# Decode attention with a gated MLP: Wq loaded as two halves on two DMA queues, with x in three pieces behind the second

## The chip, the core and the metric

The kernel runs on one core of a Trainium2 chip. A core has five engines with instruction queues of their own: TensorE (PE, with PEld for its weight loads), VectorE (DVE), ScalarE (ACT), GpSimd (POOL) and SyncE (SP). SyncE and ScalarE issue the DMAs here; each has a DMA queue, q1 for SyncE and q10 for ScalarE in the profile, and both are served by the same 16 DMA engines. The metric is the device time of one execution in microseconds. The time before is 197.39 us, the median of three runs (197.38 to 197.52).

## The reference

Eight sequences, one new token each, D = 512. The token is layer-normalised; then a grouped-query attention (32 query heads, 8 KV heads of 128) over the last W = 2048 positions of a cache of 8192, and a gated MLP, both from the same normalised token. The output joins them.

```python
xn = _layernorm(x, axis=-1)
# attention: Hq = 32, Hkv = 8, Dh = 128, W = min(4096, max(256, Sk // 4)) = 2048
q = (xn @ wq)                                   # 8 x 4096
scores = einsum("bhqd,bhkd->bhqk", q, k[last W]) * Dh ** -0.5
o = einsum("bhqk,bhkd->bhqd", softmax(scores), v[last W])
s = o @ wo
# MLP, F = 1792
h = sigmoid(xn @ w_gate) * (xn @ w_up)
g = silu(h @ w_down)
return x + s * g
```

All tensors are bfloat16. Everything that is read is read once: Wq 4 MB, the windows of K and V 32 MB each, the MLP weights 5.25 MB, Wo 4 MB, and x, which is 8 KB.

## The kernel before

The order of the instructions on each engine is the order of the program text; nothing is rescheduled. An engine works through its instructions in that order and stops at the first whose inputs are not there.

**Loads.** All large loads are issued by SyncE through the helper `load` (L115), each as one DMA over 128 partitions: Wq with 32 KB per partition, each of the eight K tiles (4 MB) with 32 KB per partition, each of the sixteen V tiles (2 MB) with 16 KB. The tiles live in two rings. The K ring (`KRING = 3` buffers) holds, in this order, Wq, K0 to K7, the gate and up weights, the down weights and Wo; the V ring has four buffers for V0 to V15. `issue_loads()` issues loads in a fixed order (K0 to K6, V0, V1, K7, V2, ...) for as long as the next one's buffer has been released. At the start it issues K0 and K1 right after Wq. K2 takes Wq's buffer, which is released after the projection (L436); K3 takes K0's, released after the last `qk` of K0; K4 takes K1's, and so on.

**x.** Before any of this ScalarE issues x in four pieces of 128 columns (L124 to L128): eight rows of 256 bytes each.

**From x to the first K tile.** VectorE casts x (L240), takes mean and variance (L242, L244), ScalarE takes the root (L248), VectorE scales (L253), PE transposes (L263), VectorE copies the transposed token (L281), and PE multiplies it with Wq in 32 matmuls (L401). `q_out(0)` then lays the first half of q out in `qz_sb`: a cast on ScalarE (L415), a 32x32-block transpose on VectorE (L420), and small copies on both (L430, L432). Two clears of 0.48 us follow on VectorE (L450 and L648).

**The loop.** For each step t, `k_turn(t)` transposes one eighth of a K tile in place on VectorE (L460), eight steps to a tile; `qk(t - 4)` multiplies it with `qz_sb` on PE (L475). After step t = 1 `q_out(1)` lays out the second half of q. After every tile VectorE takes a maximum (L489), and after four tiles comes a softmax. From t = 52 the products with V (`pv`, L605) run beside it. All `k_turn`s stand behind `q_out(0)` on VectorE, so K0 can be transposed only when x has gone through the whole chain above.

**The end.** The MLP runs late, in the gaps. Wo is loaded last, in six pieces (the last of 128 KB), each multiplied as it lands (L719); two vector operations and the output DMA close the kernel (L730 to L734).

In the profile the tiles `x2_ps` and `x2_sb` appear as `x_ps` and `x_sb`, since the numbers of buffers are left out of names.

Of the kernel before, what the change touches and what calls it, by code (L numbers as in the profile page):

```python
# [10 lines left out]
def kernel(  # L11
# [14 lines left out]
    P = 128  # L26
    B, _, D = A_x.shape
    _, Hkv, Sk, Dh = A_k_cache.shape
    Hq = A_wq.shape[1] // Dh
# [3 lines left out]
    KT = D // P  # L33
# [76 lines left out]
    queues = [nc.sync, nc.scalar]  # L110

    def load(dst, src, q=None):
        if q is None:
            q = nc.sync
        q.dma_start(out=dst, in_=src)  # L115

    def k_tile(shape, name):
        return kring.tile(shape, bf16, name=name, tag="kring", align_bytes=ALIGN)

    def v_tile(shape, name):  # L120
        return vring.tile(shape, bf16, name=name, tag="vring", align_bytes=ALIGN)

    x_bf = work.tile([B, D], bf16, name="x_bf")
    for c in range(4):  # L124
        nc.scalar.dma_start(
            out=x_bf[:, P * c : P * (c + 1)],
            in_=A_x.flatten_outer_dims()[:, P * c : P * (c + 1)],
        )  # L128

    wq_sb = k_tile([P, KT, Hq * Dh], "wq_sb")  # L130
    load(wq_sb[:], A_wq.rearrange("(p kt) n -> p kt n", kt=KT))

    k_tiles = {}
    v_tiles = {}
# [77 lines left out]
    def issue_loads():  # L212
# [36 lines left out]
        out=rstd[:], in_=mv[:, 1:2], func=AF.Sqrt, bias=eps_t[:], scale=1.0  # L249
# [4 lines left out]
        out=xn_bf[:],  # L254
# [7 lines left out]
    for kt in range(KT):  # L262
        nc.tensor.transpose(  # L263
            out=xnT_ps[:, kt, :], in_=xn_bf[:B, kt::KT], identity=ident[:B, :B]
        )
    x2_ps = psum1.tile([NCOL * 32, DC], f32, name="x2_ps", tag="misc")
    for c in range(NCOL):
# [18 lines left out]
        out=HR[:],  # L286
        in_=ident[:].rearrange("m (h q r) -> m h r q", q=NQ, r=rep),
# [6 lines left out]
        out=Qm[:],  # L294
        in_=ident[:].rearrange("m (h q r) -> m q h r", q=NQ, r=rep),
# [6 lines left out]
        out=Hm[:],  # L302
        in_=ident[:].rearrange("p (a gl) -> p gl a", gl=GL),
# [6 lines left out]
    for j in range(GL):  # L310
        for gg in range(NG):
            g = NG * gg + j // 2
            nc.gpsimd.tensor_copy(
                out=spread[:, gg, j % 2, :, j], in_=ident[:, 32 * g : 32 * g + PP]
# [5 lines left out]
        out=rows_of[:],  # L320
        in_=ident[:].rearrange("p (a m) -> p m a", m=w),
# [5 lines left out]
        out=Sel[:], in_=rows_of[:].rearrange("p (g c r) -> p c g r", g=GL, c=NCH)  # L327
# [5 lines left out]
    for gg in range(NG):  # L333
        rows = slice(32 * gg, 32 * (gg + 1))
        cols = slice(NE * GL * rep * gg, NE * GL * rep * (gg + 1))
        for e in range(NE):
            nc.gpsimd.tensor_copy(
                out=pick[rows, e, cols].rearrange("p (h d) -> p h d", d=NE)[:, :, e],
                in_=ident[rows, 32 * gg : 32 * gg + GL * rep],
# [393 lines left out]
    for c in range(NCOL):  # L733
        queues[c].dma_start(  # L734
            out=out.flatten_outer_dims()[:, DC * c : DC * (c + 1)],
            in_=y_bf[32 * c : 32 * c + B, :],
# [31 lines left out]
```

## Time and profile before

| | us |
|---|---|
| median of three runs | 197.39 |
| the profiled execution's own time | 197.33 |
| its span (first to last instruction) | 195.5 |
| PE busy | 100.9 (52%) |
| VectorE busy | 105.5 (54%) |
| ScalarE busy | 31.0 (16%) |
| x issued / cast by VectorE | 0.73 / 12.93 |
| Wq issued / landed | 0.74 / 13.04 |
| projection (L401) | 15.96 to 19.45 |
| K0 landed / first transpose | 22.63 / 22.66 |
| last V products start | 179.7 |
| output issued | 193.25 |

The span leaves out some 1.8 us of the execution's own time, at its two ends. Times inside the span count from its start. The part of the profile with the span in 40 slices gives busy shares in tenths, the mean busy share of the 16 DMA engines, and what they moved. A DMA packet in the records is one row of a transfer (a partition's contiguous bytes) or one 4-byte completion marker; each of the engines that takes part in a DMA writes a marker behind its rows.

### The profile page before, as it was taken

How to read it: one execution, taken by the hardware profiler on the slowest of the kernel's cores; microseconds unless marked ns; L12 is line 12 of the kernel's file. 1: busy time of each engine (PE TensorE's matmuls, PEld its weight loads, DVE VectorE, ACT ScalarE, POOL GpSimd, SP SyncE). 2: the span in 40 equal slices, each digit the busy share in tenths (PEclk: the TensorE clock that was granted, in tenths of full speed). 3: DMA queues.
4: the chain of work that ended last, by engine and by line, in shares of the span. 5: the costliest groups of instructions: out<-in, count | busy, mean ns of one | idle time of the engine just before them, and what ended most of it. 6: DMA issues, size and time to landing. Idle time of an engine off the chain costs nothing.

```text
span 195.5 us, 1889 instructions
## 1 busy us (share of the span) xinstructions
PE 100.9 (52%) x750; PEld 36.4 (19%) x750; DVE 105.5 (54%) x149; ACT 31.0 (16%) x69; POOL 4.6 (2%) x25
## 2 busy tenths in 40 slices
PE   0008014434333248503793989868636862585663
PEld 0002001111001012101120223321312121232452
DVE  0025899999899999999959725413100010040401
ACT  2002450000000084000011134521111114011000
POOL 8000000000000000000000000000000000000000
PEclk9999855555555556755596699999987999589969
DMA  6999999999999999999999999999999999999991
GB/s 228 430 436 442 436 456 449 429 436 427 422 442 429 429 429 429 396 422 466 429 412 432 429 429 432 427 429 429 436 429 432 432 416 438 434 425 432 423 383 34
DMA packets 5000, 81.14 MB, mean 415 GB/s; under 512 B 624, under 2 KB 896, under 8 KB 1152
## 3 DMA queue, kind: packets, MB, share of 16 engines
q1 hardware_dynamic: 4912, 81.01, 97.0%
q8 instruction: 6, 0.10, 0.2%
q10 hardware_dynamic: 80, 0.01, 0.0%
q14 instruction: 2, 0.02, 0.0%
HBM read 81.01 MB, written 0.01 MB: 414 GB/s over the span
## 4 chain that ended last, share of the span: by engine, by line
DMA 65%; DVE 19%; PE 12%; issue 1%; SPq 1%; DVEq 0%
DMA k_sb<-in_A_k_cache_dram 31%; DMA wo_sb<-in_A_wo_dram 17%; DMA v_sb<-in_A_v_cache_dram 17%; DVE k_sb L460 16%; PE acc_ps L605 5%; PE s_ps L475 3%; PE a_ps L719 3%; PE pT_ps L536 1%; DVE pt_bf L523 1%; SPq L115 1%; DVE mx L489 1%; DVE qz_sb L430 0%; DVE qT_sb L420 0%; DVE prod L730 0%; DVE y_bf L732 0%
## 5 line engine op out<-in xcount | busy, mean ns | idle before, releaser
L460 DVE STREAM_TRANSPOSE k_sb<-k_sb 128x1024 f32<-128x1024 f32 x64 | 73.7, 1210 | 3.4 <-DMA k_sb<-in_A_k_cache_dram 3.4
L475 PE MATMUL s_ps<-k_sb,qz_sb 128*32 128x512 bf16 x256 | 30.4, 576 | 51.0 <-DVE k_sb L460 45.2
L605 PE MATMUL acc_ps<-v_sb,pT_sb 128*64 128x512 bf16 x256 | 36.6, 417 | 11.2 <-DMA v_sb<-in_A_v_cache_dram 11.2
L640 DVE TENSOR_TENSOR o_sb<-o_ps,rden 16x512 bf16<-16x512 f32 (+2 forms) x6 | 3.0, 504 | 47.6 <-PE o_ps L631 47.6
L619 ACT COPY acc_sb<-acc_ps 128x512 f32<-128x512 f32 x16 | 9.4, 585 | 83.9 <-PE acc_ps L605 83.9
L475 PEld LDWEIGHTS <-qz_sb 128*32 128x32 bf16 x256 | 8.6, 117 | 75.4 <-issue 51.7
L605 PEld LDWEIGHTS <-pT_sb 128*64 128x64 bf16 x256 | 12.7, 114 | 31.2 <-DMA v_sb<-in_A_v_cache_dram 15.4
L631 PE MATMUL o_ps<-acc_sb,Sel 128*16 128x512 f32 (+2 forms) x48 | 16.3, 490 | 3.4 <-ACT acc_sb L619 3.4
L557 DVE TENSOR_SCALAR pT_sb<-pc_bf,Hm 128x1024 bf16<-128x1024 bf16 x16 | 6.6, 477 | 4.8 <-PE acc_ps L605 4.7
L263 PE MATMUL xnT_ps<-ident,xn_bf 8*128 8x8 bf16 x4 | 0.3, 175 | 15.4 <-DVE xn_bf L253 15.4
L503 ACT ACT_TABLE_LOAD x1 | 1.3, 1283 | 39.7 <-DVE nm L497 39.7
L240 DVE CAST x_f<-x_bf 8x512 f32<-8x512 bf16 x1 | 0.4, 415 | 12.9 <-DMA x_bf<-in_A_x_dram 12.9
L489 DVE TENSOR_REDUCE mx<-s_ps 128x1 f32<-128x512 f32 x8 | 5.3, 662 | 3.8 <-PE s_ps L475 3.8
L631 PEld LDWEIGHTS o_ps<-acc_sb,Sel 128*16 128x16 f32 x48 | 4.7, 105 | 14.0 <-issue 8.1
L719 PE MATMUL a_ps<-wo_sb,o_sb 128*32 128x256 bf16 x64 | 5.2, 328 | 2.9 <-DMA wo_sb<-in_A_wo_dram 2.8
L536 PE MATMUL pT_ps<-pt_bf,spread 128*128 128x512 bf16 x16 | 5.8, 479 | 1.2 <-DVE pt_bf L523 0.7
L432 ACT COPY qz_sb<-qT_sb 32x32 bf16<-32x32 bf16 x20 | 4.8, 241 | 4.8 <-DVE qT_sb L420 4.5
L351 PE MATMUL d_ps<-wgu_sb,xnT_sb 128*32 128x448 bf16 x32 | 2.6, 463 | 5.6 <-DMA wgu_sb<-in_B_w_up_dram 3.3
L503 ACT ACTIVATE p_bf<-s_ps,nm 128x512 bf16<-128x512 f32 x8 | 5.4, 685 | 0.0
L544 ACT CAST pc_bf<-pT_ps 128x512 bf16<-128x512 f32 x8 | 4.6, 585 | 4.3 <-DVE pt_bf L523 2.8
L719 PEld LDWEIGHTS <-o_sb 128*32 128x32 bf16 x64 | 4.3, 116 | 3.8 <-issue 3.2
L523 DVE STREAM_TRANSPOSE pt_bf<-p_bf 128x512 bf16<-128x512 bf16 x8 | 4.9, 666 | 0.0
(59 smaller groups left out, 38.8 us busy)
## 6 DMA issues: line engine op xcount, KB each, us to landing
k_sb<-in_A_k_cache_dram SPq DMA_DIRECT2D x8, 4096.0 KB, 19.6
v_sb<-in_A_v_cache_dram SPq DMA_DIRECT2D x16, 2048.0 KB, 16.6
wq_sb<-in_A_wq_dram SPq DMA_DIRECT2D x1, 4096.0 KB, 12.3
wo_sb<-in_A_wo_dram SPq DMA_DIRECT2D x1, 2048.0 KB
wgu_sb<-in_B_w_gate_dram SPq DMA_DIRECT2D x1, 1792.0 KB
wgu_sb<-in_B_w_up_dram SPq DMA_DIRECT2D x1, 1792.0 KB
wd_sb<-in_B_w_down_dram SPq DMA_DIRECT2D x1, 1792.0 KB
wo_sb<-in_A_wo_dram SPq DMA_DIRECT2D x1, 1024.0 KB, 34.8
```

The source lines that it names most:

```text
L432: nc.scalar.copy(out=out, in_=in_)
L460: nc.vector.transpose(out=kw, in_=kw)
L475: nc.tensor.matmul(s_tiles[i][32 * g : 32 * (g + 1), :], lhsT=qz_sb[:, hb, h, 2 * a + e, :], rhs=kT[:, :, a, h, :, e], start=(n == 0), sto ...
L489: nc.vector.reduce_max(out=mx_of[hb][:, kq : kq + 1], in_=s_tiles[i][:], axis=AX.X)
L503: nc.scalar.activation(out=p_bf[:, :, kq], in_=s_tiles.pop(NK * hb + kq)[:].rearrange("p (o c j) -> p c j o", o=2, j=NC), func=AF.Exp, bia ...
L523: nc.vector.transpose(out=pt[:, w * n : w * (n + 1)], in_=p_bf[:, w * n : w * (n + 1)])
L536: nc.tensor.matmul(pT_ps[:], lhsT=spread[:, gg, y].rearrange("p k g -> p (k g)"), rhs=pt[:, c, y, :], start=(y == 0), stop=(y == 1), skip_ ...
L557: nc.vector.tensor_scalar(out=pT_of[hb, gg][:, :, gl, :], in0=pc, scalar1=Hm[:, gl : gl + 1], scalar2=None, op0=ALU.mult,)
L605: nc.tensor.matmul(acc_tiles[i][w * c : w * (c + 1), :], lhsT=pT[:, GL * rep * ch : GL * rep * ch + w], rhs=v_tiles[i][:, ch : ch + NCH, : ...
L619: nc.scalar.copy(out=acc_sbs[i // NSUM][:, i % NSUM], in_=acc_tiles.pop(i)[:])
L631: nc.tensor.matmul(o_ps[rows, :n, :], lhsT=Sel[:, c].rearrange("p g r -> p (g r)"), rhs=acc_sb[:, :, Dh * c : Dh * (c + 1)], start=(c == 0 ...
L719: nc.tensor.matmul(a_ps[32 * c : 32 * (c + 1), :], lhsT=o2_sb[:, k, :], rhs=wo_parts[k][:, DC * c : DC * (c + 1)], start=(k == 0), stop=(k ...
```

## The change

Wq's tile is allocated first. Its load is cut in two by `kt`, the outer half of each partition's 32 KB: the first 16 KB of each partition are issued by SyncE, the second 16 KB by ScalarE. x's loads, still on ScalarE, now stand behind that second half, and are three in place of four: columns 0 to 255 in one piece of 512-byte rows, then 256 to 383 and 384 to 511. Nothing else in the program differs; the matmuls of L401 read the same tile, and now wait for both halves.

```diff
+    wq_sb = k_tile([P, KT, Hq * Dh], "wq_sb")
+    wq_rows = A_wq.rearrange("(p kt) n -> p kt n", kt=KT)
+    for n, q in enumerate(queues):
+        kts = slice(KT // 2 * n, KT // 2 * (n + 1))
+        load(wq_sb[:, kts, :], wq_rows[:, kts, :], q)
+
     x_bf = work.tile([B, D], bf16, name="x_bf")
-    for c in range(4):
+    for c0, c1 in ((0, 2), (2, 3), (3, 4)):
         nc.scalar.dma_start(
-            out=x_bf[:, P * c : P * (c + 1)],
-            in_=A_x.flatten_outer_dims()[:, P * c : P * (c + 1)],
-        )
-
-    wq_sb = k_tile([P, KT, Hq * Dh], "wq_sb")
-    load(wq_sb[:], A_wq.rearrange("(p kt) n -> p kt n", kt=KT))
+            out=x_bf[:, P * c0 : P * c1],
+            in_=A_x.flatten_outer_dims()[:, P * c0 : P * c1],
+        )
```

`queues` is `[nc.sync, nc.scalar]`.

## The prediction

> **What bounds the kernel now.** I read the slices of the span first, then the queues, then the chain of waits, then the timelines of VectorE and SyncE around the first K loads.
>
> ```profile
> DMA  6999999999999999999999999999999999999991
> GB/s 228 430 436 442 436 456 449 429 436 427 422 442 429 429 429 429 396 422 466 429 412 432 429 429 432 427 429 429 436 429 432 432 416 438 434 425 432 423 383 34
> ...
> q1 hardware_dynamic: 4912, 81.01, 97.0%
> ...
> q10 hardware_dynamic: 80, 0.01, 0.0%
> ```
>
> The 16 DMA engines are full from the first slice to the last; q1 (SyncE's loads) takes 97.0% of them. So 81.01 MB at about 430 GB/s set the time: an edit loses only by leaving the engines empty somewhere, and gains only by starting that stream sooner. q10 is ScalarE's queue: today x and half of the output.
>
> What keeps the stream full is SyncE issuing each load before the last one is through. Wq, K0 and K1 fill the three K buffers; K2 needs Wq's buffer, and K3 needs K0's, free once K0 is transposed and multiplied. The chain of waits and SyncE's timeline (start, length) say when:
>
> ```profile
> 33.33 1.92 PE s_ps L475 x15
> 35.26 0.02 issue
> 35.27 17.72 DMA k_sb<-in_A_k_cache_dram
> ...
> 19.50 0.54 SPq L115 DMA_DIRECT2D k_sb<-in_A_k_cache_dram  x1
> ...
> 44.88 0.53 SPq L115 DMA_DIRECT2D k_sb<-in_A_k_cache_dram  x1
> ...
> 54.49 0.54 SPq L115 DMA_DIRECT2D k_sb<-in_A_k_cache_dram  x1
> ...
> 64.80 0.53 SPq L115 DMA_DIRECT2D k_sb<-in_A_k_cache_dram  x1
> ```
>
> K2 goes out at 19.50, K3 at 35.27, K4 to K6 at 44.88, 54.49 and 64.80. When would the engines be empty? A load ends on each engine with a 4-byte completion marker; the window 41.1 to 41.75 us holds all 16 of K2's:
>
> ```profile
> DMA packets 32, 0.52 MB, mean 807 GB/s; under 512 B 16, under 2 KB 16, under 8 KB 16
> ```
>
> In finer windows the first falls at 41.13. So K3 went out 5.86 us before it was needed. VectorE, which frees K0, has almost no room of its own (its timeline, idle time before each group in brackets):
>
> ```profile
> 12.93 0.41 DVE L240 CAST x_f<-x_bf 8x512 f32<-8x512 bf16 x1 [12.93 <-DMA x_bf<-in_A_x_dram]
> ...
> 21.58 0.48 DVE L648 MEMSET o_sb<- 128x512 uint32 x1
> 22.66 2.37 DVE L460 STREAM_TRANSPOSE k_sb<-k_sb 128x1024 f32<-128x1024 f32 x2 [0.59 <-DMA k_sb<-in_A_k_cache_dram]
> ...
> 53.09 4.62 DVE L460 STREAM_TRANSPOSE k_sb<-k_sb 128x1024 f32<-128x1024 f32 x4 [0.59 <-DMA k_sb<-in_A_k_cache_dram]
> ...
> 101.38 4.62 DVE L460 STREAM_TRANSPOSE k_sb<-k_sb 128x1024 f32<-128x1024 f32 x4 [2.22 <-DMA k_sb<-in_A_k_cache_dram]
> ```
>
> It starts when x lands (12.93), works through layernorm, projection copies and memsets to 22.06, waits 0.59 for K0, and then runs almost without a break: waits for K loads come to 0.59 + 0.59 + 2.22 = 3.4 us in all. A later x makes VectorE later by the same, less 0.59.
>
> **What sets x's arrival.** x is 8 KB and lands only at 12.93, beside Wq (13.04 = 0.74 + 12.3 from its issue). The queues in four neighbouring windows (6.5 to 7.2, to 7.8, to 8.4, to 9.0 us; packets, MB, share) show why:
>
> ```profile
> q1 hardware_dynamic: 1, 0.03, 10.8%
> ...
> q1 hardware_dynamic: 15, 0.49, 189.5%
> q10 hardware_dynamic: 8, 0.00, 0.8%
> ...
> q1 hardware_dynamic: 1, 0.03, 12.6%
> ...
> q1 hardware_dynamic: 15, 0.49, 189.5%
> q10 hardware_dynamic: 8, 0.00, 1.5%
> ```
>
> Each x piece is 8 rows, one on each of 8 engines, plus a marker on each. On such an engine one entry of q10 passes, then one 32 KB row of Wq (1.21 us: between 28.2 and 30.62 us, 32 rows pass, two per engine in 2.42), then the next entry. The two queues take turns entry by entry, whatever an entry's size. x's first piece went ahead of Wq; the other three, 6 entries, each waited one row, and the last passed with Wq's last row.
>
> **The change, part by part.**
>
> Wq in two halves: SyncE's ring now holds A1..A8 (16 KB rows per engine) and a marker, then K0's eight 32 KB rows; ScalarE's holds B1..B8 and a marker. Bytes are the same and the rows alternate, so Wq ends where it did. V moves in 16 KB rows at the same 430 GB/s, so the smaller row costs nothing in the stream. PE's projection waits for both halves and for x.
>
> Issuing: ScalarE issues four DMAs as before, B in place of one x piece. Its four took 1.70 us; B's issue lies between 0.30 (the shortest of x) and 0.61 (the longest of SyncE). Behind it on ScalarE stand a table load, which ended at 3.74, and the square root, which waits on x; both have 10 us of cover. Nothing on POOL or PE is moved past a queue.
>
> x in three pieces behind B: three pieces are 6 entries, and all stand behind B's 9. x's last entry is the 15th of its ring. Taking turns, SyncE's ring has by then passed 8 rows, a marker and six K0 rows (five if ScalarE's ring goes first). Today x's last entry passes when Wq's last row ends; now it passes 6 x 1.21 = 7.28 us after that. x lands at 12.93 + 7.28 = 20.21.
>
> Which ring leads, and by how much, the trace does not show. Bounds: x's first piece, issued at 0.73, passed before Wq, issued at 0.74, so ScalarE may lead; its second, issued 0.6 us after Wq, found three Wq rows ahead of it, so a late start costs up to three turns. So three to nine K0 turns; a ninth turn meets only K0's marker, so x waits for three to eight rows: 3.6 to 9.7 us. I take 6, the even start with SyncE first, as ScalarE's first issue took 0.58 us and SyncE's 0.39.
>
> Then, step by step:
> - VectorE reaches K0's first transpose at 22.06 + 7.28 = 29.34 in place of 22.66: 6.69 late. PE's projection, done near 19.45, ends at 26.7 and K2 is issued then; it is needed at 31.45 (41.13 less one load of 9.68), so K2 is covered.
> - K3 is issued at 35.27 + 6.69 = 41.96. From issue to a full-speed row takes 1.62 us (Wq: issued 0.74, its first row through by 3.57, less the row's own 1.21), so K3's slack is 5.86 - 1.62 = 4.24 us, and the engines stand empty for 6.69 - 4.24 = 2.45 us. Between 1.08 (the bare wait to the first packet of x or Wq is near 1.0) and 2.2 (the slowest engine) for that start, the hole is 1.9 to 3.0.
> - No second hole. The next loads are needed 9.68 us apart (50.81, 60.49, 70.17), and 2.45 later than that from now on. K4's and K5's slacks are 4.31 and 4.38, plus 2.45: more than 6.69. At K3 VectorE no longer waits 0.59, so it is 6.10 late at K6's issue, and K6 has 70.17 - 64.80 - 1.62 + 2.45 = 6.20. Close, but covered. K7 was out 10 us early, V4 likewise; by V6 (issued 111.93, needed near 118.7) VectorE has eaten the 2.22 too and is 3.9 late.
> - After the K loads PE waits for V and the end waits for Wo, so the whole tail moves by the hole, 2.45.
>
> Sum: the profiled execution's 197.33 (span 195.5 and 1.8 around it; the median is 0.06 higher) + 2.45 = 199.8 us. For n rows waited the hole is 1.21 n - 0.59 - 4.24: 0 at four, 1.23 at five, 2.45 at six, 3.66 at seven, 4.87 at eight.
>
> The Trainium skill's "DMA: Bandwidth & Descriptors", section "Queues, rings and completion order", says an engine takes turns between queue rows by packets, of some 9 to 17 descriptors. By that rule a turn would carry all of B, and x's entries would leave together. The trace has one row to a turn in every window above, so the sum doesn't use it; it stands behind two rivals.
>
> **The rivals.**
> *No change, 197.3 us.* If x waits for four K0 rows or fewer, VectorE is at most 1.21 x 4 - 0.59 = 4.26 us late and K3's slack of 4.24 swallows it. It needs ScalarE's ring to lead by two turns or more, or B and x to leave in one long turn. For it: x's first piece did beat Wq. Against it: the two issues started 0.01 us apart, and turns were single. 0.14.
> *Slower still, 202.2 us.* SyncE's ring leads by two or more turns, or x waits a whole K0 (the other outcome of long turns). For it: the three rows ahead of x's second piece. Against: that piece was issued 0.6 us later, B is not. 0.17, some of it beyond 202.2, as x entries that reach K1's rows wait further turns.
> *Faster, about 196.7 us.* The first Wq rows took until 3.57 where 1.75 + 1.21 = 2.96 would do; if two rings opened at once hid that 0.6 us and x still came in time, the stream would start sooner. For it: nothing but that slow row. Against: all engines read from the same moment either way. 0.05.
>
> **How the numbers follow.** Five to seven rows (198.6 to 201.0) hold the remaining 0.64, with six the likeliest: 199.8. The range must reach down to no change and up to eight rows: 197.1 to 202.2. About 0.2% (0.4 us) is what a measurement can tell from no change: faster 0.05, same 0.13, slower 0.82.
>
> **What would show it.** On VectorE, the first x cast at 19 to 21.5 us in place of 12.93, and no wait for K0 before its first transpose; in the windows after Wq, q10 entries alternating with K0's rows, six turns; K3's issue near 42; one slice near 42 to 44 us with DMA well under 9 and all others full; K3 landing near 55.4 with no wait of VectorE before its transposes. If x is cast before 18, the count of turns is wrong; if the hole is there but a second one follows near 72, K6's cover was misjudged; if x is late and there is no hole, the slack was.

## The result, and the profile after

The changed kernel takes 202.26 us, the median of five runs (201.61 to 202.99), beside 197.51 (197.38 to 197.57): a ratio of 1.0245, 95% interval 1.0216 to 1.0274. The profiled execution took 202.0 us with a span of 200.2, 4.7 more than the span before. The forecast was 199.8 with a range up to 202.2: right in direction, and half the loss.

The page of the changed kernel, the span in 40 slices (5.0 us each) and the two queues:

```profile
DMA  6999999969999999999999999999999999999980
GB/s 232 435 472 420 432 419 419 426 203 414 396 386 432 426 426 445 416 426 458 419 426 422 429 426 435 430 429 426 439 432 429 422 435 428 439 420 427 433 361 20
...
q1 hardware_dynamic: 4912, 78.91, 92.9%
q10 hardware_dynamic: 208, 2.11, 2.5%
```

The stream that was full has one slice at 203 GB/s, the ninth (40 to 45 us), and a weaker pair, the eleventh and twelfth, at 396 and 386 (50 to 60 us). ScalarE's queue q10 now carries the second half of Wq.

VectorE's timeline in the changed kernel (start, length, idle time before a group in brackets):

```profile
20.24 0.41 DVE L243 CAST x_f<-x_bf 8x512 f32<-8x512 bf16 x1 [20.24 <-DMA x_bf<-in_A_x_dram]
...
29.40 2.37 DVE L463 STREAM_TRANSPOSE k_sb<-k_sb 128x1024 f32<-128x1024 f32 x2
...
45.03 9.11 DVE L463 STREAM_TRANSPOSE k_sb<-k_sb 128x1024 f32<-128x1024 f32 x8
...
54.64 9.11 DVE L463 STREAM_TRANSPOSE k_sb<-k_sb 128x1024 f32<-128x1024 f32 x8
```

x is cast at 20.24 in place of 12.93. The groups of transposes have no bracket any more: VectorE, 6.74 us late at the first of them, never waits for a K load again. SyncE's timeline has the issues of K3 to K6:

```profile
42.02 0.54 SPq L115 DMA_DIRECT2D k_sb<-in_A_k_cache_dram  x1
...
51.62 0.54 SPq L115 DMA_DIRECT2D k_sb<-in_A_k_cache_dram  x1
...
61.23 0.54 SPq L115 DMA_DIRECT2D k_sb<-in_A_k_cache_dram  x1
...
70.84 0.54 SPq L115 DMA_DIRECT2D k_sb<-in_A_k_cache_dram  x1
```

What the DMA engines did around K3's issue shows in two neighbouring windows, 41.1 to 41.95 and 41.95 to 43.3 us:

```profile
DMA packets 16, 0.00 MB, mean 0 GB/s; under 512 B 16, under 2 KB 16, under 8 KB 16
...
DMA packets 0, 0.00 MB, mean 0 GB/s; under 512 B 0, under 2 KB 0, under 8 KB 0
```

The first holds the 16 completion markers of K2 and nothing else; in the second nothing begins at all. K3's rows begin from 43.34 on. Two-microsecond stretches of the changed kernel (busy times of PE, its loads, VectorE, ScalarE, GpSimd; granted clock; DMA share; GB/s) show a second weak place:

```profile
40.00:42.00 2.00, 1.90 (x16) 0.63 (x16) 2.00 (x3) 0.00 (x0) 0.00 (x0) 1.00 0.57 246
42.00:44.00 2.00, 0.00 (x0) 0.00 (x0) 2.00 (x3) 0.00 (x0) 0.00 (x0) 1.00 0.68 180
44.00:46.00 2.00, 1.41 (x16) 0.63 (x16) 2.00 (x3) 0.00 (x0) 0.00 (x0) 1.00 0.75 279
...
54.00:56.00 2.00, 1.81 (x16) 0.60 (x17) 2.00 (x4) 0.00 (x0) 0.00 (x0) 1.00 1.13 410
56.00:58.00 2.00, 0.09 (x4) 0.00 (x0) 2.00 (x2) 0.00 (x0) 0.00 (x0) 1.00 0.73 279
58.00:60.00 2.00, 0.71 (x8) 0.31 (x11) 2.00 (x3) 0.00 (x0) 0.00 (x0) 1.00 1.10 475
```

Shares over 1 and single low stretches also come from rows of 1.2 us being put down where they start, so I read the holes from the markers, found with finer windows. On the engine that comes first, K2 ends at 41.16 and a K load takes 9.68 us; K3 ends at 53.72, which is 53.72 - 41.16 - 9.68 = 2.88 late. K4 ends at 64.32, another 0.92 late (64.32 - 53.72 - 9.68). K5 and all later loads follow at full pace.

### The profile page after: what moved, and what is told of

Its sections match the earlier page's. It is cut to its first block, busy times and chain, and to the rows that moved or that the text cites. A ratio compares the mean times of both kernels' runs of the same rounds, so it can differ in the third digit from the quotient of the medians.

```text
span 200.2 us, 1886 instructions
## 1 busy us (share of the span) xinstructions
PE 101.9 (51%) x750; PEld 37.0 (18%) x750; DVE 105.2 (53%) x149; ACT 30.8 (15%) x69; POOL 4.6 (2%) x25
## 3 DMA queue, kind: packets, MB, share of 16 engines
q10 hardware_dynamic: 208, 2.11, 2.5%
## 4 chain that ended last, share of the span: by engine, by line
DVE 43%; DMA 42%; PE 10%; issue 2%; ACTq 1%; SPq 1%; ACT 0%; DVEq 0%
DVE k_sb L463 34%; DMA v_sb<-in_A_v_cache_dram 17%; DMA wo_sb<-in_A_wo_dram 16%; DMA x_bf<-in_A_x_dram 9%; PE acc_ps L608 4%; PE a_ps L722 3%; DVE mx L492 2%; DVE pT_sb L560 2%; PE pT_ps L539 1%; DVE pt_bf L526 1%; DVE qz_sb L433 1%; PE s_ps L478 1%; PE q_ps L404 1%; DVE qT_sb L423 1%; SPq L115 1%
## 5 line engine op out<-in xcount | busy, mean ns | idle before, releaser
L608 PE MATMUL acc_ps<-v_sb,pT_sb 128*64 128x512 bf16 x256 | 37.2, 421 | 11.3 <-DMA v_sb<-in_A_v_cache_dram 11.3
```

The costliest lines, as they stand in the source:

```text
L608: nc.tensor.matmul(acc_tiles[i][w * c : w * (c + 1), :], lhsT=pT[:, GL * rep * ch : GL * rep * ch + w], rhs=v_tiles[i][:, ch : ch + NCH, : ...
```

## The experiments

Three theories were tried. A is the prediction's: x's turns make VectorE late, K3 goes out late, the stream has one hole. B is A with another price for a late load, read from the trace after. C is the rival that two rings for Wq cost time by themselves. A load's lead below is the time from its issue to the first completion marker of the load in front of it; its loss is the lateness of its own first marker, as just worked out. A load has a marker on each of the 16 engines, and the last of them can be later than the first by more than before; where that matters the last marker is given too.

**One, two and four pieces of x behind the half.** The only edit is the list of pieces, `((0, 2), (2, 3), (3, 4))` in the changed kernel:

```diff
-    for c0, c1 in ((0, 2), (2, 3), (3, 4)):
+    for c0, c1 in ((0, 4),):
```

With two pieces it is `((0, 2), (2, 4))`, with four `((0, 1), (1, 2), (2, 3), (3, 4))`.

> Edit of the changed kernel: x as one piece behind the second Wq half, so two q10 entries in place of six. Theory A (the turns make x late, K3 goes out late, the stream has holes): x waits two K0 rows, VectorE casts it near 12.93 + 2.43 = 15.4 us, K3 goes out near 37.1, 4 us before it is needed; no hole, 197.4 us, within 0.3 of before. Theory B (as A, but a load must go out some 3.1 us ahead of need, as the changed kernel's K4 and K5 suggest: 2.1 ahead lost 0.9, 3.1 ahead lost nothing): also 197.4. Theory C (two rings for Wq disturb the stream by themselves): still 201 to 202.

> x as two pieces behind the second Wq half: four q10 entries. A with the prediction's slack of 4.24 us: cast near 17.8, VectorE 4.26 us late, K3 out near 39.5 and just covered: 197.4 us. B: K3 goes out 1.6 us ahead of need, short of 3.1; read between the changed kernel's two holes (0.9 lost at 2.1 ahead, 2.9 lost at 0.9 too late) it loses 1.2 at K3 and 0.1 to 0.2 at K4: 198.7 to 199.3. C: 201 to 202.

> x as four pieces behind the second Wq half: eight q10 entries, the count of the kernel before, at the new place. Cast near 12.93 + 9.70 = 22.6 by A and B, VectorE 9.1 us late, K3 out near 44.4. A with the prediction's slack: one hole of 4.87, 202.2 us. B: a hole of 3.25 + 2.05 = 5.3 at K3 and about 0.9 at K4, and the slowest DMA engine up to 0.75 further behind: 203.6 to 204.4. C: about as the changed kernel, 202.3, whatever the pieces.

| pieces | x cast | K3 issued | lead | loss at K3 | loss at K4 | median, us | ratio to before (95%) |
|---|---|---|---|---|---|---|---|
| one | 15.50 | 37.27 | 3.90 | 0.10 | 0.00 | 197.70 | 1.0007 (0.9997 to 1.0016) |
| two | 17.93 | 39.72 | 1.46 | 0.56 | 0.62 | 199.95 | 1.0121 (1.0104 to 1.0138) |
| three (the change) | 20.24 | 42.02 | -0.86 | 2.88 | 0.92 | 202.26 | 1.0245 (1.0216 to 1.0274) |
| four | 22.95 | 44.72 | -3.46 | 5.46 | 1.23 | 204.95 | 1.0373 (1.0341 to 1.0404) |

Each piece moves the cast by 2.3 to 2.7 us, two turns of 1.21 and a little. One piece costs nothing that can be told from no change, so C is out. A with the prediction's slack falls at two pieces: it gave 197.4, the kernel took 199.95. B had the sign, and was too low as well: 198.7 to 199.3, and 203.6 to 204.4 for four. At two pieces the first markers lose 0.56 and 0.62, together 1.2, in sum about what B said. What B left out is the last engine: K3's first marker (51.42) is 0.6 later than in the kernel before, its last (54.89) is 2.3 later.

**V0 into the hole.** x stays as late as in the changed kernel; only the order of the loads is changed:

```diff
+    loads.remove((1, 0))
+    loads.insert(loads.index((0, 3)), (1, 0))
     loads[-2:-2] = [(2, 0)]
```

> The changed kernel as it is, x late as it is, but V0 (2 MB, its buffer is free) is issued between K2 and K3, where the hole was; V1 and all else stay. x is cast near 20.2 and K3 goes out near 42.0 as in the changed kernel, but is needed 4.86 us later, at 46.0; K4 to K7 have 4 us or more. A and B: the stream has no hole and the time is back at 197.4 us. C: stays at 201 to 202.

Measured: 197.79 us, the median of ten runs from 197.48 to 199.33, ratio 1.0029 (1.0006 to 1.0052). x is cast at 20.27, K3 goes out at 42.05, as late as in the changed kernel, and the slices of its page no longer show the hole:

```profile
GB/s 226 432 446 446 439 445 439 425 386 460 422 425 425 425 452 432 439 412 462 439 389 432 396 429 422 432 430 432 429 429 432 429 428 432 430 432 430 423 310 16
```

K3, now with a lead of 3.96, loses nothing. So nearly all of the 4.75 us is the stream running dry, and not VectorE's lateness as such. The trace is of one of the longer runs, 198.97 us, 1.64 more than the profiled run of the kernel before. In it V4, issued at 106.56 with a lead of 2.45, loses 0.35, and the markers of the last V load span 3.09 us in place of 1.84. How much of this the run at the median has is not known.

**The halves alone, and the lateness alone.** In the first, x is loaded in one piece ahead of the second half. In the second, Wq is one load as before, x's loads on ScalarE's queue are taken out, and x goes on SyncE's queue between K0 and K1. The first edit is shown against the changed kernel, the second against the kernel before:

```diff
+    x_bf = work.tile([B, D], bf16, name="x_bf")
+    for c0, c1 in ((0, 4),):
+        nc.scalar.dma_start(
+            out=x_bf[:, P * c0 : P * c1],
+            in_=A_x.flatten_outer_dims()[:, P * c0 : P * c1],
+        )
+
     wq_sb = k_tile([P, KT, Hq * Dh], "wq_sb")
     wq_rows = A_wq.rearrange("(p kt) n -> p kt n", kt=KT)
...
-    x_bf = work.tile([B, D], bf16, name="x_bf")
-    for c0, c1 in ((0, 2), (2, 3), (3, 4)):
...
```

```diff
-    for c in range(4):
-        nc.scalar.dma_start(
...
     def load_k(i):
+        if i == 1:
+            load(x_bf[:], A_x.flatten_outer_dims())
         hb, kq = divmod(i, NK)
```

> The halves alone: Wq on two queues as in the changed kernel, but x ahead of the second half on ScalarE's queue, in one piece. A and B: x is there within 4 us; the second half stands two entries back and ends two or three K0 rows (2.4 to 3.6 us) after the first, so the projection starts near 15.5 to 17 in place of 15.96 and VectorE is at most 1 us late, inside K3's lead of 5.86: 197.4 us. C (the two rings cost by themselves): above 200.

> The lateness alone: Wq whole on SyncE as in the kernel before, nothing on ScalarE's queue, and x in one piece on SyncE's queue between K0 and K1. x lands right behind K0 and is cast near 22.7, as with four pieces behind the half (22.95, which took 204.95). A and B: the same time as that, 204 to 205.5. C: 197.4, as there are no halves.

The halves alone take 197.52 us beside 197.46, ratio 1.0000 (0.9991 to 1.0009), with x cast at 2.22. Of the projection, 8 matmuls ran at 10.56 and the other 24 from 17.78, later than the 15.5 to 17 expected; VectorE's first transpose is at 23.04, 0.38 late. The lateness alone takes 205.60, ratio 1.0412 (1.0395 to 1.0430). Its cast, in VectorE's timeline, and its slices:

```profile
22.82 0.41 DVE L237 CAST x_f<-x_bf 8x512 f32<-8x512 bf16 x1 [22.82 <-DMA x_bf<-in_A_x_dram]
```

```profile
DMA  7999999919989999999999999999999999999980
GB/s 270 444 418 412 433 470 380 425 45 392 431 312 439 425 431 437 421 418 447 434 421 418 434 431 421 437 423 437 431 421 444 421 432 424 437 430 433 413 324 10
```

Two holes (45 and 312 GB/s) like those of four pieces behind the half (45 and 333) stand there with no load on a second queue; by the first markers K3 loses 5.35 and K4 1.31. This separates the causes: the halves cost nothing, x's place costs everything. The Trainium skill, "DMA: Bandwidth & Descriptors", section "Issuing engines are not separate DMA queues", says that DMAs from several engines run on the same 16 DMA engines and interleave, and that issuing from more than one saves only issue time; the halves alone agree.

**K0 in 16 KB rows.** K0 is loaded as two DMAs, each half of a partition's 32 KB; x's six entries stay.

```diff
+        parts = 2 if i == 0 else 1
+        w = KC * Dh // parts
+        for n in range(parts):
+            load(dst[:, w * n : w * (n + 1)], src[:, :, w * n : w * (n + 1)])
```

> The changed kernel with K0 as two loads of 16 KB rows in place of one of 32 KB rows; the bytes and x's six entries stay. If the queues take turns entry by entry (A and B), each x entry now waits 0.61 us: x is cast near 12.93 + 3.64 = 16.6, K3 goes out near 38.4, 2.8 us ahead of need, where 2.79 ahead lost 0.08: 197.4 to 198.0. If turns go by bytes or by time, x stays near 20.2 and the time at 202.

```profile
15.95 0.42 DVE L245 CAST x_f<-x_bf 8x512 f32<-8x512 bf16 x1 [15.95 <-DMA x_bf<-in_A_x_dram]
```

x is cast at 15.95, five turns of 0.61 after 12.93 (one fewer than expected), and K3 goes out 3.43 us ahead: a turn is one row, whatever its size. The profiled execution, 197.68 us, has no hole. The time was expected at 197.4 to 198.0; the median of ten runs is 198.92 (197.68 to 199.59), ratio 1.0064 (1.0041 to 1.0088). So the expectation of the time was missed, and the trace is of the shortest of the ten.

**The later K loads in 16 KB rows.** The same edit with `i >= 2`, so that x's turns stay and K2 to K7 change.

> The changed kernel with K2 to K7 as two loads each of 16 KB rows; Wq, K0, K1 and x stay, so x is cast near 20.2 and K3 goes out near 42.0. B as a count of rows (an engine needs two rows behind the one it writes): two rows of 0.61 and 1.0 from the issue make 2.2 us of lead, so K4 (2.1 ahead) loses near nothing in place of 0.9, and the time is 201.0 to 201.5. B as a latency that the row's size does not change: K4 loses 0.6 to 1.2 again, 202.3. A: one hole of 2.45, 199.8, which the changed kernel itself already contradicts.

Measured: 202.90 us, ratio 1.0280 (1.0233 to 1.0327). x is cast at 20.31 and K4, with a lead of 1.97, loses 1.0 again, where B as a count of rows had it lose near nothing. Rows of half the size do not shorten the lead that a load needs, so it is not a number of rows. The traced run is one of the longer (203.62; two others took 202.2), and its last V load's markers span 3.73 us.

**Two kernels once more, for their traces.**

> The changed kernel once more, for its trace; its five runs lay between 201.6 and 203.0 where the kernel before lies within 0.2. If the spread comes from x's turns, the cast of x moves from 20.24 by steps of 1.2 us and K3's issue with it. If it comes from the DMA engines being out of step after a hole (first and last completion marker of a K load 0.7 us apart before the first hole, 2.1 after it, 2.6 at the end), the cast and K3's issue (42.02) stay within 0.1 and the time follows the last marker.

> The changed kernel with K0 in 16 KB rows once more; its ten runs lay between 197.7 and 199.6, and the profiled one (197.68, x cast at 15.95, K3 out 3.4 us ahead of need) showed no hole. By x's turns: a slower run has x cast 0.6 to 1.8 us later. By engines out of step: the cast stays at 15.95 and a slower run has markers of K3 or later further apart than 1.8 us.

The changed kernel took 202.4 us, with x cast at 20.17 and K3 issued at 41.92, the same six turns. Holes: 2.70 and 1.14. Its engines end further apart, 2.9 us between the first and the last marker of V15 where the other trace has 2.6. So, between these two at least, a difference in time does not come from x's turns. But K3's markers span only 1.06 us here, behind a hole of nearly the same size, where they span 2.11 in the other trace, so the hole alone does not set them apart. K0 in 16 KB rows took 197.9, with x cast at 16.22, a lead of 3.20 and again no hole. Neither trace of that kernel is of a run near 199; why it takes 199 in some runs stays open.

## Why the prediction was wrong

- *"The two queues take turns entry by entry ... x lands at 12.93 + 7.28 = 20.21."* Right: x is cast at 20.24, after the six rows that were taken. In the changed kernel each of x's six entries shows as eight packets of q10 beside 14 of q1; two of the six windows, 14.4 to 15.0 and 15.6 to 16.2 us:

```profile
q1 hardware_dynamic: 14, 0.46, 176.9%
q10 hardware_dynamic: 8, 0.00, 0.8%
...
q1 hardware_dynamic: 14, 0.46, 176.9%
q10 hardware_dynamic: 8, 0.00, 1.5%
```

  The rule of the Trainium skill that the prediction set beside it ("DMA: Bandwidth & Descriptors", "Queues, rings and completion order": turns of some 9 to 17 descriptors) does not describe these queues; one row passes per turn here.
- *"VectorE ... 6.69 late", "K3 is issued at ... 41.96".* Right: 29.40 for 29.34, and 42.02.
- *"From issue to a full-speed row takes 1.62 us", hence a hole of 2.45.* Mis-sized: the hole is 2.88, inside the stated 1.9 to 3.0. K3's first rows start 1.3 to 2.2 us after the issue and take 1.7 to 2.3 us each in place of 1.21. With the engines idle, the price from issue to full speed is loss + lead: 2.88 - 0.86 = 2.0, and with four pieces 5.46 - 3.46 = 2.0. The 1.62 came from the first Wq rows of the earliest engine.
- *"No second hole."* This is the step that failed. It took 1.62 us for a sufficient lead, and found 4.31 + 2.45 = 6.76 against 6.69, cover by a hair. The hole that it named as a risk, at K6, did not come; K6 lost nothing. K4 went out 2.10 us before K3's first marker and still lost 0.92: from issue to full speed it paid 3.0 us with the engines at work, where K3 paid 2.0 on idle ones and the prediction reckoned with 1.62 for both. Leads and losses over the traces: 3.1 to 4.1 us, at most 0.12; 2.8, 0.1; 2.45, 0.35; K3 with two pieces, 1.46, 0.56; K4 behind a late K3, 2.0 to 2.1, 0.6 to 1.3. K5, with 3.09, lost nothing, as the hole at K4 had given it the lead.

  The lead alone does not set the loss. K2 stands behind a load that came in time. With four pieces it was issued with a lead of 2.16, in the kernel with the lateness alone with 1.87; its first marker lost 0.03 and 0.07, its last 0.9 and 2.0. So a part of K4's loss may belong to the late K3 in front of it. No run has K4 with 2.1 us of lead behind a K3 in time, and why K4 pays 3.0 stays open.
- *"The whole tail moves by the hole."* Short by 0.75. The first engine's markers are 3.83 late from K4 to the end, but a load lands with its last engine. The last V load's markers span 1.84 us before and 2.58 after. The first multiplication with Wo, in the timelines before and after, has moved by 4.54:

```profile
187.25 5.21 PE L719 MATMUL a_ps<-wo_sb,o_sb 128*32 128x256 bf16 x64 [2.84 <-DMA wo_sb<-in_A_wo_dram]
```

```profile
191.79 5.34 PE L722 MATMUL a_ps<-wo_sb,o_sb 128*32 128x256 bf16 x64 [2.88 <-DMA wo_sb<-in_A_wo_dram]
```

  What sets the engines apart is shown in part, and it is not the hole alone. In the kernel before, with no late load, the span of the markers grows from 0.55 us at K2 to 1.75 at K3. Between these markers the DMA engines also carry two fetches of the program's own instructions, 8 KB in 0.31 us and 16 KB in 0.94 (the queues q14 and q8, in the window 47 to 49 us):

```profile
q8 instruction: 1, 0.02, 2.9%
q14 instruction: 1, 0.01, 1.0%
```

  In the changed kernel the span grows from 0.71 to 2.11 at K3, with two such fetches (0.31 and 0.97 us) ahead of K3's last marker. From K4 to V4 it stays at 1.9; at V5 it grows by 0.62, and a 16 KB fetch starts at 119.38, just ahead of V5. That this fetch falls on an engine that is already behind is argued from the times alone, since the records name no engine.
- The rivals: eight rows of waiting gave 202.2, the right time for another reason. No change and faster are out.

The sum as it should have stood: 197.33 + 2.88 + 0.92 + 0.75 = 201.9, beside the profiled 202.0. The second trace of the same kernel gives 197.33 + 2.70 + 1.14 + 1.07 = 202.2, beside 202.4. The 0.75 and 1.07 are the growth of the last V load's span, which differs from run to run.

## What to carry to other kernels

A small load behind a large one waits twice per piece, once for its row and once for its marker, and each time for a whole row of whatever the other queue holds; put it ahead, or in one piece, or beside small rows. Where a stream of loads sets the time, ask of each how long before its need it is issued: 3.1 us and more cost at most 0.12 on the first engine here, and about 2 us (1.9 to 2.2) cost 0.03 to 1.3 on the first engine and up to 2.0 on the last. When an early step becomes late, a load whose buffer is already free, moved into the gap, can give the time back.

## What was not expected of the hardware

A load that was issued 2.1 us before the stream needed it still slowed the stream, and halving its rows did not help (K4 lost 1.0 in 16 KB rows, 0.9 and 1.1 in 32 KB rows). The 16 DMA engines can fall out of step and stay so: in the kernel before, with no hole, a load's markers span 0.55 us up to K2, 1.75 from K3 on, at two instruction fetches, and still 1.84 at the last V load. A load that is issued late while the engines are at work can do it too: in the kernel with the lateness alone K2, with a lead of 1.87 and no fetch near it, takes the span from 0.83 to 2.75. The changed kernel's five runs spread over 1.4 us, where the kernel before spread over 0.2 in five runs and 0.7 in 19 others. Holes do not explain this: the kernel with the lateness alone has two and its four runs spread over 0.4, K0 in 16 KB rows has none in either trace and its ten runs spread over 1.9. The cause of the spread stays open.
